# All 16 retention units in front of the first feed-forward layer

## Chip, cores and metric

The kernel runs on one core of a Trainium2 chip. The metric is the time of one execution on the device in microseconds (us), as the median of three runs. Engines are called PE (TensorE, the matrix engine), PEld (its weight loads, which overlap with it), DVE (VectorE), ACT (ScalarE), POOL (GpSimd) and SP (SyncE, which issues the DMAs).

## What is computed

A retention layer with 4 batches, 8 heads, 576 positions and 64 columns per head feeds two feed-forward layers over 2304 tokens of 512 columns, the first 2048 wide with a sigmoid gate, the second 1024 wide with a softmax, a product and a layer norm.

```python
def _attn_ref(q, k, v):
    scores = scale * np.matmul(q, k.transpose(0, 1, 3, 2))
    gamma = 1.0 - 2.0 ** (-5.0 - np.arange(H, dtype=np.float32))
    rel = pos[:, None] - pos[None, :]
    Dmat = np.where(rel >= 0, gamma[:, None, None] ** rel[None, :, :], 0.0)
    return np.matmul(scores * Dmat[None], v)
def _moe_ref(x, w_in, w_out):
    h = x @ w_in
    return (h * (1.0 / (1.0 + np.exp(-1.702 * h)))) @ w_out
def _moe2_ref(x, w_in, w_out, g_ln):
    h = x @ w_in
    solu = h * softmax(h)
    return (layer_norm(solu) * g_ln) @ w_out
```

## The kernel before

**Retention.** A unit is one batch and one pair of heads; there are 16. Its 576 positions are four chunks of 128 and a rest of 64. Within a chunk the scores k times q are computed directly and masked by a triangle; what earlier chunks contribute goes through a state of 64 x 64 per head, the sum of k times v over those chunks. The decay is carried by factors: v is multiplied by gamma to the minus position, the output by gamma to the position, over the whole 576 positions. The stages of a unit are `st0` (v times its factors, L308, on DVE for units 0, 1, 2 and 7, else on POOL), `st2` (scores, L356, and the two masks, L360), `states` (k times v of each chunk, L318, and the copy out by ACT, L327, into the two diagonal blocks of a 128 x 128 matrix per chunk), `st1` (running sums of the states over the chunks, L336, on DVE for units 0 to 2, else on POOL) and `st4` (states times q as full 128 x 128 matmuls, L376 and L380; masked scores times v, L385; the rest of 64 positions, L396; the scores of the next unit's rest, L344; and on DVE the output times its factors, L403 and L404). A table of output factors for 576 positions is grown on ACT from one for 128 (L197).

The stages of neighbouring units overlap: the scores of unit u come before `st4` of unit u - 1, and `st4` of u - 1 has the states of u in its middle. Inputs of a unit (128 x 2240 numbers) lie in one of six slots; when `st4` of a unit is written, the load of a later unit into its slot is issued on SP's queue.

**First layer.** 2304 tokens are six blocks of 384, and 2048 columns are two halves of eight slices. A step is one block and one slice: `emit_h` (12 matmuls, L439, then a sigmoid on ACT, L443, a product on DVE, L444, and a split of the result into a high part, L446 on ACT or L448 on DVE, and a low part, L449) and `emit_y` of the step before (12 matmuls, L470). Weights and tokens are split likewise, so that three products of rounded parts stand for one in full precision. Weights arrive as 64-bit numbers, 128 x 1024 words for half a slice. Six pieces on DVE (L224, L227, L230 for each half) convert a slice to 32 bits; then ACT casts the high part (L246) and POOL subtracts for the low part (L251, two instructions). `split_x` makes the parts of the tokens (L420 on ACT, L421 on POOL).

**What sets the order.** Each engine runs its instructions in the order in which the program writes them. Conversion pieces and the weight casts wait in a list, and `background(n)` writes n pieces of DVE and whatever follows them. The table `START` says how many pieces follow each stage and how many retention stages are written between the steps of the first block; later blocks take the rest in even portions. Units 0 to 3 come before the first step, the other twelve are spread over the first four blocks (`attend`).

**Second layer.** It starts after both halves of the first (L499 onwards) and isn't touched.

Of the kernel before, what the change touches and what calls it, by code (L numbers as in the profile page):

```python
# [9 lines left out]
F32 = mybir.dt.float32  # L10
F32R = mybir.dt.float32r
U32 = mybir.dt.uint32
# [33 lines left out]
for _name, _w in (  # L46
    ("vdec", NP * NV), ("tri", CH), ("tri2", LAST), ("half", 1), ("g_ln", FB), ("step", NP * NCH), ("qdec", NP * CH),
):
    _CC[_name] = (_n, _n + _w)
    _n += _w  # L50
# [3 lines left out]
def constants():  # L54
# [10 lines left out]
    step = np.zeros((P, NP, NCH))  # L65
    vdec = np.zeros((P, NP, NV))
    j = np.arange(P)
    for p in range(NP):
        g = gamma[2 * p + head_of_row][:, None]
        qdec[:, p] = g ** j[None, :]  # L70
        step[:, p] = g ** (CH * np.arange(1, NCH + 1)[None, :])
        for b in range(NCH):
            for a in range(2):
                vdec[:, p, 2 * b + a] = gamma[2 * p + a] ** (-(b * P + j))
        vdec[:, p, NV - 1] = gamma[2 * p + head_of_row] ** (-(NCH * CH + j % D))
# [17 lines left out]
for _name, _w in (  # L93
    ("c", _CC["qdec"][0]), ("qdec", NP * S), ("y", NB * KB * TB), ("g", 2 * TB), ("x", B * NP * S // 2),
    ("att", 2 * CATT + 2 * NCH * P + 4 * NCH * CH + 2 * LAST), ("t", SLICE),
):
    _M[_name] = _n
    _n += _w
# [3 lines left out]
IN_AT = [_M["att"], _M["att"] + CATT, _M["y"] + 3 * YT, _M["y"] + 3 * YT + CATT, CMEM, CMEM + 4 * S]  # L102
IN_OF = [0, 1, 2, 3, 4, 5, 0, 1, 2, 3, 0, 1, 2, 3, 0, 1]
ST_AT = _M["att"] + 2 * CATT
R1_AT = ST_AT + 2 * NCH * P
R2_AT = R1_AT + 4 * NCH * CH

T_START = [_M["t"], _M["y"] + 1 * YT, _M["y"] + 2 * YT]
# [13 lines left out]

START = {
    "warm": 10,
    "load": ["u1a", "u1b", "q", "u2a", "u2b", "u3a", "w0a", "u3b", "u4a", "w0b", "u4b", "w1a", "w1b", "u5a", "u5b", "w2a", "w2b", "w3a", "w3b", "w4a", "w4b"],
    "pre": [0, 0, 0, 0, 0, 1, 2, 0, 0, 2, 1, 3, 1],
    "ahead": [3],  # L130
    "step": [[2, 1, 2], [2, 1, 2], [2, 1, 2], [2, 1, 2], [2, 1, 2], [2, 2, 2], [2, 2, 2], [2, 0, 4]],
    "stages": [1, 0, 1, 0, 1, 1, 1, 1, 0, 2, 1, 1, 1, 1, 1, 1],
    "per_stage": 1,
    "lo_dve": [0, 0, 1, 0, 0, 0, 0, 0],
    "hi_act": [0, 1, 0, 0, 1, 0, 1, 1],
    "lo_at": [0, 4],
    "v_dve": [0, 1, 2, 7],
    "sum_dve": [0, 1, 2],
}


class Build:
# [37 lines left out]
    def load_qdec(self):  # L180

        nc = self.nc
        q = self.qdec()
        nc.sync.dma_start(
            out=q[:, :, 0:CH],
            in_=self.const_in[:, _CC["qdec"][0]:].rearrange("r (p i) -> r p i", p=NP),
        )

    def qdec(self):
        return self.at(_M["qdec"], NP * S).rearrange("r (p i) -> r p i", p=NP)  # L190

    def grow_qdec(self, p):
        q = self.qdec()
        for c in range(1, NCH + 1):
            n = min(CH, S - c * CH)
            f = self.const("step")[:, p * NCH + c - 1:p * NCH + c]
            self.nc.scalar.mul(q[:, p, c * CH:c * CH + n], q[:, p, 0:n], f)  # L197
# [5 lines left out]
    def load_unit(self, u, part=None):  # L203

        t = IN_AT[IN_OF[u]]
        a, b = {None: (0, CATT), 0: (0, 2 * CH), 1: (2 * CH, CKN), 2: (CKN, CATT), 3: (0, CKN)}[part]
        self.load(t + a, self.att_in[u, :, a:b])
# [57 lines left out]
    def stage(self, i, u):  # L265
        getattr(self, f"st{i}")(u)
        self.staged.add((i, u))

    def un(self, u):

        t = self.at(IN_AT[IN_OF[u]], CATT)
        st = self.at(ST_AT + (u % 2) * NCH * P, NCH * P).rearrange("r (c e) -> r c e", c=NCH)
# [10 lines left out]
    def qd(self, u):  # L283
        return self.qdec()[:, u % NP]

    def bank(self, name):
        return self.ps.tile([P, 512], F32, tag="s", name=name, bufs=4)

    def banks(self, u, name):

        if u < NP:
            t = self.ps.tile([P, 2, 512], F32, tag="y", name=f"{name}_{u}", bufs=2)
            return [t[:, a] for a in range(2)]
        return [self.bank(f"{name}{a}_{u}") for a in range(2)]
# [7 lines left out]
    def st0(self, u):  # L302

        v = self.un(u)[0][:, CV:CATT].rearrange("r (b e) -> r b e", b=NV)
        p = u % NP
        dec = self.const("vdec")[:, p * NV:(p + 1) * NV].unsqueeze(2).to_broadcast([P, NV, D])
        eng = self.nc.vector if u in START["v_dve"] else self.nc.gpsimd
        eng.tensor_tensor(v, v, dec, ALU.mult)  # L308

    def states(self, u):  # L310

# [12 lines left out]

        for a in range(2):
            r = slice(a * D, (a + 1) * D)
            nc.scalar.copy(st[r, :, r], pt[r, 0:NCH * D].rearrange("r (c e) -> r c e", c=NCH))  # L327

    def st1(self, u):

        if u == 0:
            self.states(0)
# [14 lines left out]
    def st2(self, u):  # L347
# [3 lines left out]
        s = self.banks(u, "s1")  # L351

        for c in range(NCH):
            for a in range(2):
                r = slice(a * D, (a + 1) * D)
                nc.tensor.matmul(  # L356
                    s[a][:, c * CH:(c + 1) * CH], self.k(t, c, r), self.q(t, c, r), start=True, stop=True
# [457 lines left out]
```

## Time and profile before

| | us |
|---|---|
| median of three runs | 736.18 (734.79 to 737.37) |
| the profiled execution | 738.06 |
| its span, first to last instruction | 736.30 |
| PE busy in the span | 711.4 (97%) |
| DVE, POOL, ACT busy | 445.1, 203.9, 185.8 |

PE is busy nearly throughout, but busy time is time with a matmul in flight at whatever clock the engine had. The granted clock is given per stretch as a share of 2.4 GHz; its two levels are 1.00 and 0.50 (1.2 GHz), and a value between is a mean. Rows of the timeline give the start and the duration of a run of instructions; a run that starts before the last one's end overlaps it, so costs are read from one start to the next. In the trace each matmul of the program shows as two instructions where both its operands are in 32-bit floating point (retention), and as one where they are split parts (the layers).

### The profile page before, as it was taken

What the parts mean: (1) busy time and instruction counts of PE and PEld (TensorE: products, weight loads), DVE (VectorE), ACT (ScalarE), POOL (GpSimd) and SP (SyncE); (2) the same over time, 40 slices, a digit from 0 to 9 for tenths busy, and PEclk for the clock granted to TensorE, in tenths of its full rate; (3) what the DMA queues carried; (4) which work ended last, traced back from release to release, by engine and by line L of the source; (5) the groups of instructions that cost most, each with busy time, mean ns of one, the idle gap of its engine ahead of it and who ended that gap; (6) DMA issues with size and microseconds to landing.
All of it is one profiled execution on the core that took longest, in us unless ns stands there. A gap on an engine that the chain in (4) does not pass through costs nothing.

```text
span 736.3 us, 10807 instructions
## 1 busy us (share of the span) xinstructions
PE 711.4 (97%) x4380; PEld 660.6 (90%) x4380; DVE 445.1 (60%) x745; ACT 185.8 (25%) x372; POOL 203.9 (28%) x211
## 2 busy tenths in 40 slices
PE   8888899999999999989999999999999999999998
PEld 7777799999999998989999999999878888888887
DVE  5899834443534789944676767655577454645451
ACT  3331231221212133412111111224323232222231
POOL 1576860312312026712021111137412111111000
PEclk9797999999999999999999999999999999999999
DMA  9980130111010333200112112000000000000001
GB/s 329 416 359 1 64 126 1 63 64 63 1 58 1 115 115 115 86 29 1 58 58 85 59 58 59 31 0 1 1 1 28 29 16 28 16 28 28 15 29 43
DMA packets 13392, 49.37 MB, mean 67 GB/s; under 512 B 1440, under 2 KB 2592, under 8 KB 11680
## 3 DMA queue, kind: packets, MB, share of 16 engines
q1 hardware_dynamic: 13344, 48.70, 18.3%
q8 instruction: 34, 0.56, 0.3%
q14 instruction: 14, 0.11, 0.0%
HBM read 43.97 MB, written 4.72 MB: 66 GB/s over the span
## 4 chain that ended last, share of the span: by engine, by line
PE 84%; DVE 12%; issue 2%; ACT 1%; DMA 1%; SPq 0%; POOL 0%; DVEq 0%; ACTq 0%
PE h L439 25%; PE yp L470 25%; PE o L561 14%; PE h L499 12%; PE zT L534 2%; DVE mem L224 2%; DVE mem L230 2%; PE o L385 2%; DVE wraw L227 2%; PE s L356 1%; PE o L376 1%; DVE gs L449 1%; PE T L318 1%; DVE mem L444 1%; DMA mem<-in_att 1%
## 5 line engine op out<-in xcount | busy, mean ns | idle before, releaser
L470 PE MATMUL yp<-gs,w 128*128 128x384 f32 x1152 | 222.6, 341 | 4.6 <-DVE gs L449 2.3
L439 PE MATMUL h<-xs,w 128*128 128x384 f32 x1152 | 224.2, 344 | 0.0
L470 PEld LDWEIGHTS yp<-gs,w 128*128 128x128 f32 x1152 | 205.7, 191 | 7.2 <-DVE gs L449 3.2
L439 PEld LDWEIGHTS h<-xs,w 128*128 128x128 f32 x1152 | 207.3, 191 | 1.1
L444 DVE TENSOR_TENSOR mem<-h,mem 128x384 f32<-128x384 f32 x96 | 53.4, 557 | 143.1 <-ACT mem L443 142.9
L443 ACT ACTIVATE mem<-h 128x384 f32<-128x384 f32 x96 | 47.3, 493 | 281.9 <-PE h L439 278.1
L561 PE MATMUL o<-w,zs 128*128 128x512 f32 (+1 forms) x456 | 105.3, 387 | 0.0
L499 PE MATMUL h<-w,ys 128*128 128x512 f32 x432 | 101.3, 391 | 1.0 <-DVE mem L516 0.8
L499 PEld LDWEIGHTS h<-w,ys 128*128 128x128 f32 x432 | 80.9, 188 | 19.0 <-DVE mem L516 1.0
L561 PEld LDWEIGHTS o<-w,zs 128*128 128x128 f32 x456 | 81.3, 188 | 17.2
L251 POOL TENSOR_TENSOR w<-mem,w 128x512 fp32r<-128x512 f32 x48 | 69.3, 1463 | 37.2 <-ACT w L246 35.6
L449 DVE TENSOR_TENSOR gs<-mem,gs 128x384 fp32r<-128x384 f32 x89 | 64.0, 719 | 8.9 <-DVE gs L448 0.5
L421 POOL TENSOR_TENSOR xs<-xb,xs 128x384 fp32r<-128x384 f32 (+1 forms) x32 | 27.7, 894 | 146.9 <-ACT xs L420 146.9
L421 POOL TENSOR_TENSOR xs<-mem,xs 128x384 fp32r<-128x384 f32 (+1 forms) x32 | 27.7, 886 | 113.3 <-ACT xs L420 113.3
L544 DVE TENSOR_TENSOR zs<-zT,zs 128x512 fp32r<-128x512 f32 x36 | 23.1, 684 | 46.9 <-ACT zs L543 46.9
L448 DVE CAST gs<-mem 128x384 fp32r<-128x384 f32 x92 | 45.6, 495 | 8.7
L522 POOL TENSOR_TENSOR mem<-mem 128x1 f32<-128x1 f32 x18 | 9.9, 550 | 122.3 <-DVE mem L521 122.3
L246 ACT CAST w<-mem 128x1024 fp32r<-128x1024 f32 x24 | 25.0, 1048 | 50.4 <-DVE mem L230 28.9
L515 DVE TENSOR_TENSOR mem<-h,mem 128x1024 f32<-128x1024 f32 x18 | 22.1, 1227 | 23.6 <-ACT mem L514 23.6
L487 POOL TENSOR_TENSOR ys<-mem,ys 128x512 fp32r<-128x512 f32 x18 | 23.8, 1320 | 43.1 <-ACT ys L486 43.1
L336 POOL TENSOR_TENSOR mem<-mem 128x128 f32<-128x128 f32 x39 | 22.2, 570 | 38.5 <-ACT mem L327 36.5
L514 ACT ACTIVATE mem<-h,mem 128x1024 f32<-128x1024 f32 x18 | 20.1, 1118 | 48.6 <-DVE mem L512 48.6
(80 smaller groups left out, 577.8 us busy)
## 6 DMA issues: line engine op xcount, KB each, us to landing
mem<-in_att SPq DMA_DIRECT2D x10, 1120.0 KB, 5.4
mem<-in_w SPq DMA_DIRECT2D x16, 512.0 KB, 3.7
wraw<-in_w SPq DMA_DIRECT2D x10, 512.0 KB, 10.6
out<-mem SPq DMA_DIRECT2D x17, 256.0 KB, 2.0
mem<-in_w2in SPq DMA_DIRECT2D x8, 512.0 KB, 3.8
mem<-in_w2out SPq DMA_DIRECT2D x8, 512.0 KB, 3.7
wraw<-in_w SPq DMA_DIRECT2D x3, 1024.0 KB, 16.0
mem<-in_att SPq DMA_DIRECT2D x4, 544.0 KB, 8.4
```

What stands on the lines that cost most here:

```text
L246: nc.scalar.copy(self.w[key][0], w)
L251: nc.gpsimd.tensor_tensor(lo[:, c], w[:, c], f32(hi[:, c]), ALU.subtract)
L421: nc.gpsimd.tensor_tensor(t[:, 1, done:done + n], x, f32(t[:, 0, done:done + n]), ALU.subtract)
L439: nc.tensor.matmul(h[:, 0:TB], a[:, w], x[:, b], start=(n == 0), stop=(n == 3 * KB - 1))
L443: nc.scalar.activation(g, h[:, 0:TB], AF.Sigmoid, scale=1.702)
L444: nc.vector.tensor_tensor(g, h[:, 0:TB], g, ALU.mult)
L448: nc.vector.tensor_copy(gs[:, 0], g)
L449: lo_engine.tensor_tensor(gs[:, 1], g, f32(gs[:, 0]), ALU.subtract)
L470: nc.tensor.matmul(o, a[:, w], gs[:, b], start=(first and i == 0), stop=(last and i == 2))
L487: nc.gpsimd.tensor_tensor(ys[:, 1], y, f32(ys[:, 0]), ALU.subtract)
L499: nc.tensor.matmul(h[:, n], ys[:, a, k], b[:, w], start=(i == 0), stop=(i == 3 * KB - 1))
L561: nc.tensor.matmul(o[:, 0:n], z[:, a, k], b[:, c:c + n], start=(k == 0 and i == 0), stop=(k == FB - 1 and i == 2),)
```

## The change

All 16 units are done before the first step of the first layer; `START`, `attend` and the grown table are gone. In each unit:

- The factors run within a chunk only. v of all chunks takes the same two columns of factors, multiplied on ACT in three instructions. The output takes one table of 128 columns for all chunks.
- The state of a chunk is scaled by gamma to the 128 when ACT copies it out, and the running sums on DVE multiply by that too (`scalar_tensor_tensor`), so that the state moves from chunk to chunk.
- States are kept as 64 columns without the empty blocks, and states times q runs as two 64 x 64 matmuls for each chunk, one for each head, in two quarters of the array. They stand behind the masked scores times v and the states of the next unit.
- Five slots in place of six; with each unit one half slice of weights is loaded. Two conversion pieces are written in each unit from the second on (`PIECES`), three in each step of the first block (`STEP`). All casts of the gated result in the first block are on ACT, all low parts on DVE.

```diff
-IN_OF = [0, 1, 2, 3, 4, 5, 0, 1, 2, 3, 0, 1, 2, 3, 0, 1]
+NU = 5
+IN_AT = [_M["att"], _M["att"] + CATT] + [_M["y"] + i * CATT for i in range(3)]
...
+PIECES = (1, 1, 0)
+STEP = (1, 1, 1)
...
     def st0(self, u):
-        eng = self.nc.vector if u in START["v_dve"] else self.nc.gpsimd
-        eng.tensor_tensor(v, v, dec, ALU.mult)
+        for a in range(2):
+            w = v[:, 0:n].rearrange("r (c a e) -> r a c e", a=2, e=D)[:, a]
+            self.nc.scalar.mul(w, w, d[:, a:a + 1])
+        self.nc.scalar.mul(v[:, n:], v[:, n:], d[:, 2:3])
...
-        for a in range(2):
-            r = slice(a * D, (a + 1) * D)
-            nc.scalar.copy(st[r, :, r], pt[r, 0:NCH * D].rearrange("r (c e) -> r c e", c=NCH))
+        nc.scalar.mul(
+            st, pt[:, 0:NCH * D].rearrange("r (c e) -> r c e", c=NCH),
+            self.const("step")[:, u % NP:u % NP + 1],
+        )
...
-        eng = self.nc.vector if u in START["sum_dve"] else self.nc.gpsimd
+        g = self.const("step")[:, u % NP:u % NP + 1]
         for c in range(1, NCH):
-            eng.tensor_tensor(st[:, c], st[:, c - 1], st[:, c], ALU.add)
+            self.nc.vector.scalar_tensor_tensor(st[:, c], st[:, c - 1], g, st[:, c], ALU.mult, ALU.add)
...
-        for c in range(1, NCH):
-            nc.tensor.matmul(
-                o[:, c * CH:(c + 1) * CH], st[:, c - 1], self.q(t, c),
-                start=(c == 1), stop=False, skip_group_check=True,
-            )
...
+        if u + 1 < B * NP:
+            self.states(u + 1)
+
+        for c in range(1, NCH):
+            for r in half:
+                nc.tensor.matmul(
+                    o[r, c * CH:(c + 1) * CH], st[r, c - 1], self.q(t, c, r),
...
+        last = B * NP - 1
...
+        for u in range(1, last + 2):
+            if u <= last:
+                self.st2(u)
+                if u > 1:
+                    self.background(PIECES[0])
+            self.st4(u - 1)
+            self.staged.add((4, u - 1))
+
+            if u - 1 + NU <= last:
+                self.load_unit(u - 1 + NU)
+            load_w()
+            if u > 1:
+                self.background(PIECES[1])
+            if u <= last:
+                self.st1(u)
+            if u < last:
+                self.st0(u + 1)
+            if u - 1 < NP:
+                self.split_x(0, 0, u - 1)
```

Two places of the order. First DVE from the masks of unit 3 (before) and unit 4 (after) on; s, o are scores and outputs in PSUM with the unit as first number, wraw is a raw weight slice. Before:

```order
L360 TENSOR_TENSOR mem<-s_3_275,mem 128x512 x2
L403 TENSOR_TENSOR mem<-o_2_286,mem 128x512
L404 TENSOR_TENSOR mem<-o_2_287,mem 128x64
L345 TENSOR_TENSOR mem<-o_2_287,mem 128x64
L224 TENSOR_SCALAR mem<-wraw_96 128x512
L227 SCALAR_TENSOR_TENSOR wraw_96<-wraw_96,mem 128x512
L230 SCALAR_TENSOR_TENSOR mem<-wraw_96 128x512
```

After (in the names of the change, s has no unit in its name here):

```order
L317 TENSOR_TENSOR mem<-s_324,mem 128x512 x2
L197 SCALAR_TENSOR_TENSOR wraw_91<-wraw_91,mem 128x512
L364 TENSOR_TENSOR mem<-o_3_336,mem 128x512
L369 TENSOR_TENSOR mem<-o_3_361,mem 128x64
L302 TENSOR_TENSOR mem<-o_3_361,mem 128x64
L200 SCALAR_TENSOR_TENSOR mem<-wraw_91 128x512
L293 SCALAR_TENSOR_TENSOR mem<-mem 128x64 x3
```

The pieces now stand one by one, before and behind the output scaling, and the three sums of every unit are on DVE.

Second ACT, in the unit in which the first weight slice is complete; T are states in PSUM, w a split weight, xs split tokens. Before:

```order
L420 CAST xs_0_2_320<-mem 128x384
L197 ACTIVATE mem<-mem 128x128 x3
L197 ACTIVATE mem<-mem 128x64
L246 CAST w_333<-mem 128x1024
L327 COPY mem<-T_366 64x4x64 x2
```

After:

```order
L283 ACTIVATE mem<-T_345,mem 128x256
L216 CAST w_374<-mem 128x1024
L265 ACTIVATE mem<-mem 128x4x64 x2
L266 ACTIVATE mem<-mem 128x64
L385 CAST xs_0_3_382<-mem 128x384
```

The scaling of v for the next unit (L265, L266) stands behind the cast of the weight, as it does in every third unit.

## Rows read from the trace of the kernel before

**Rows 1.** Windows by stage: length, busy us (instructions) per engine, clock, DMA share, GB/s.

```profile
9.46:90.24 80.78, 67.91 (x600) 61.46 (x597) 73.78 (x109) 24.70 (x52) 50.80 (x44) 0.83 0.59 234
90.24:226.00 135.76, 135.76 (x1102) 131.23 (x1101) 56.01 (x109) 30.37 (x74) 38.42 (x55) 1.00 0.15 51
226.00:510.30 284.30, 280.21 (x1572) 278.95 (x1569) 192.34 (x321) 64.71 (x132) 75.02 (x68) 0.99 0.17 56
```

**Rows 2.** Windows up to 226 us, line L439, then L470, alone (PE, PEld).

```profile
0.00:226.00 226.00, 72.74 (x361) 66.03 (x361) 0.94 0.33 126
...
0.00:226.00 226.00, 67.60 (x348) 61.80 (x348) 0.94 0.33 126
```

**Rows 3.** Timeline of PE, undisturbed steps: start, us, line, instructions.

```profile
242.99 2.28 PE L439 MATMUL h<-xs,w 128*128 128x384 f32 x12
...
247.22 2.28 PE L439 MATMUL h<-xs,w 128*128 128x384 f32 x12
```

**Rows 4.** Timeline of PE, two clean units and two waits [idle before it <- releaser].

```profile
13.81 1.16 PE L356 MATMUL s<-mem 64*128 64x128 f32 x16
14.90 0.94 PE L376 MATMUL o<-mem 128*128 128x128 f32 x6
...
16.56 1.10 PE L385 MATMUL o<-mem 128*64 128x128 f32 x16
17.49 0.63 PE L318 MATMUL T<-mem 128*64 128x64 f32 x16
18.06 0.33 PE L396 MATMUL o<-mem 64*64 64x64 f32 x4
...
18.43 1.16 PE L356 MATMUL s<-mem 64*128 64x128 f32 x16
...
22.36 1.23 PE L376 MATMUL o<-mem 128*128 128x128 f32 x4 [2.34 <-DVE mem L336]
...
58.15 1.09 PE L376 MATMUL o<-xb,mem 128*128 128x128 f32 x4 [1.24 <-POOL mem L336]
```

**Rows 5.** Windows of 2 us after the two waits, columns as in rows 1.

```profile
22.00:24.00 2.00, 1.64 (x8) 1.52 (x10) 1.93 (x5) 0.00 (x0) 0.16 (x1) 0.50 1.03 422
...
60.00:62.00 2.00, 1.88 (x16) 1.48 (x16) 2.00 (x2) 0.00 (x0) 1.98 (x2) 0.50 0.00 0
```

**Rows 6.** Timeline of DVE in unit 3.

```profile
17.87 0.41 DVE L224 TENSOR_SCALAR mem<-wraw 128x512 uint32<-128x512 uint32 x1
18.20 0.68 DVE L403 TENSOR_TENSOR mem<-o,mem 128x512 f32<-128x512 f32 x1
18.80 0.21 DVE L404 TENSOR_TENSOR mem<-o,mem 128x64 f32<-128x64 f32 x1
...
19.06 0.68 DVE L227 SCALAR_TENSOR_TENSOR wraw<-wraw,mem 128x512 uint32<-128x512 uint32 x1
19.78 1.37 DVE L230 SCALAR_TENSOR_TENSOR mem<-wraw 128x512 uint32<-128x512 uint32 x1
21.07 1.23 DVE L336 TENSOR_TENSOR mem<-mem 128x128 f32<-128x128 f32 x1
```

**Rows 7.** Timeline of POOL in the same stretch.

```profile
20.56 1.59 POOL L308 TENSOR_TENSOR mem<-mem 128x576 f32<-128x576 f32 x1
```

**Rows 8.** Lines L336 and L230 up to 60 us: duration ns min/median/max, starts, forms.

```profile
L336 DVE TENSOR_TENSOR mem<-mem x9: 293/294/1230, 10.5 to 22.7; 128x128 f32<-128x128 f32 x9
...
L230 DVE SCALAR_TENSOR_TENSOR mem<-wraw x9: 693/1374/1644, 19.8 to 56.1; 128x512 uint32<-128x512 uint32 x9
```

**Rows 9.** Timeline of ACT: four multiplications by a column, and the cast of a weight.

```profile
11.73 1.23 ACT L197 ACTIVATE mem<-mem 128x128 f32<-128x128 f32 x4 [1.32 <-DMA mem<-in_consts]
...
47.34 1.04 ACT L246 CAST w<-mem 128x1024 fp32r<-128x1024 f32 x1 [6.97 <-DVE mem L230]
```

**Rows 10.** Page, part 5: two groups, with busy us, mean ns, idle before.

```profile
L444 DVE TENSOR_TENSOR mem<-h,mem 128x384 f32<-128x384 f32 x96 | 53.4, 557 | 143.1 <-ACT mem L443 142.9
L449 DVE TENSOR_TENSOR gs<-mem,gs 128x384 fp32r<-128x384 f32 x89 | 64.0, 719 | 8.9 <-DVE gs L448 0.5
```

**Rows 11.** Timeline of PE behind a wait at 313 us.

```profile
315.38 3.52 PE L470 MATMUL yp<-gs,w 128*128 128x384 f32 x10 [0.86 <-DVE gs L449]
```

More of the change, by code (lines that the diff above doesn't have):

```diff
@@ L117 @@
 T_LATER[1] = T_LATER[1] + [OB_AT, U_AT + 2 * F2]
[L126 to L139, printed above, removed]
+PIECES = (1, 1, 0)
+STEP = (1, 1, 1)
+WARM = 10
 class Build:
@@ L180, in load_qdec @@
     def load_qdec(self):
[L182 to L186, printed above, removed]
-        )
[L189 to L197, printed above, removed]
+        lo, hi = _CC["qdec"]
+        self.load(_M["c"] + lo, self.const_in[:, lo:hi])
     def const(self, name):
@@ L393, in st4 @@
             self.states(u + 1)
-        for a in range(2):
-            r = slice(a * D, (a + 1) * D)
+        for c in range(1, NCH):
+            for r in half:
+                nc.tensor.matmul(
+                    o[r, c * CH:(c + 1) * CH], st[r, c - 1], self.q(t, c, r),
+                    start=False, stop=(c == NCH - 1), skip_group_check=True,
+                )
+        o2 = self.bank(f"o2_{u}")
+        for r in half:
+            nc.tensor.matmul(
+                o2[r, 0:LAST], st[r, NCH - 1], self.q(t, NCH, r),
+                start=True, stop=False, skip_group_check=True,
+            )
+        for r in half:
             nc.tensor.matmul(
@@ L584, in run @@
                 self.load_consts()
[L586 to L603 removed]
+        self.load_unit(1, 3)
+        self.load_qdec()
+        self.load_unit(1, 2)
+        for u in range(2, NU):
+            self.load_unit(u, 3)
+            self.load_unit(u, 2)
+            load_w()
         others = []
@@ L637, in run @@
-        cut = order.index((4, NP - 1)) + 1
-        pre = [sum(1 for i, _ in order[:n] if i) for n in range(cut)]
-        for n, (i, u) in enumerate(order[:cut]):
-            run_stage(i, u)
-            if i == 4:
-                self.split_x(0, 0, u)
-            if i:
-                self.background(START["pre"][pre[n]])
-        rest = order[cut:]
-        def attend(n, pieces=0):
-            while rest and (n > 0 or not rest[0][0]):
-                i, u = rest.pop(0)
-                run_stage(i, u)
-                if i:
-                    self.background(pieces)
-                    n -= 1
@@ L656, in run @@
-        for n in START["ahead"]:
-            attend(1, n)
-        stage_no = [s for s in rest if s[0]]
-        total = len(stage_no)
-        done = lambda: total - sum(1 for i, _ in rest if i)
-        goal = [None] + [stage_no.index((4, u)) + 1 for u in (9, 12)] + [total]
+        last = B * NP - 1
+        self.st0(0)
+        self.st2(0)
+        self.states(0)
+        self.st1(0)
+        self.st0(1)
+        for u in range(1, last + 2):
[7 more added lines that the diff above has]
+                self.load_unit(u - 1 + NU)
+            load_w()
+            if u > 1:
[6 more added lines that the diff above has]
+                self.split_x(0, 0, u - 1)
+            if u > 1:
+                self.background(PIECES[2])
@@ L676, in run @@
             if start:
-                attend(START["stages"][2 * fl], START["per_stage"])
-                self.background(START["step"][fl][0])
-            elif g == 0 and j < 4:
-                if fl == 0:
-                    before = done()
-                upto = lambda slot: before + -(-(goal[j] - before) * min(slot + 1, 14) // 14) - done()
-                attend(upto(2 * fl))
+                while f not in self.split:
+                    self.background(1)
+                self.background(STEP[0])
             if have_next and fl == FH - 2:
@@ L686, in run @@
                 self.split_x(*nextb, 1)
-            lo_pool = start and not START["lo_dve"][fl]
-            self.emit_h(g, j, f, nc.gpsimd if lo_pool else nc.vector, start and START["hi_act"][fl])
-            bg = START["step"][fl][1] if start else 2
+            self.emit_h(g, j, f, nc.vector, start)
+            bg = STEP[1] if start else 2
             if fl:
@@ L694, in run @@
                 self.split_x(*nextb, 3)
-            if start:
-                attend(START["stages"][2 * fl + 1], START["per_stage"])
-            elif g == 0 and j < 4:
-                attend(upto(2 * fl + 1))
             if prev is not None:
@@ L707, in run @@
                     held.pop(0)()
-            self.background((START["step"][fl][2] if start else 1) + (0 if fl else bg))
+            self.background((STEP[2] if start else 1) + (0 if fl else bg))
             if g == NH - 1 and last_block:
@@ L715, in run @@
             prev = (g, j, f)
-        assert not rest
         self.emit_y(*prev)
```

127 lines of the change are left out of this document (47 added, 80 removed).

## Prediction

> **What bounds the kernel now.** I read the busy time by stage first [rows 1]. From 90.24 us on, TensorE (PE) works without a gap: 135.76 of 135.76 us, then 280.21 of 284.30, at a granted clock of 1.00 and 0.99. In 9.46 to 90.24 it works 67.91 of 80.78 us at a mean clock of 0.83, while VectorE (DVE) is busy 73.78 of 80.78. So the tail is PE's own time, and the start is the only place where 10 us or more can be won. Second, how much of the start is the feed-forward layer. Up to 226.0 us (the stages are cut where the scores of unit 1 start, 9.46, and where the last retention matmul ends, 226.0) the trace has 30 groups of 12 matmuls of the h kind and 29 of the y kind (361 and 348 instructions [rows 2], one of them already in the next group). A step of h and y takes 247.22 - 242.99 = 4.23 us where nothing disturbs it [rows 3], so a group takes 2.115 us, and the 59 groups would take 59 x 2.115 = 124.8 us. **The rest, 226.0 - 124.8 = 101.2 us, is what the 16 retention units, the start and every loss cost today.** The changed kernel does the same 59 groups after its front, so it wins what its front (and any new loss in the first block) stays under 101.2 us. Everything behind 226.0 us has the same instructions in the same order, its own stall at 313 us included [rows 11], and is costed at no change.
>
> Third, why the start loses. Two units pass cleanly: the scores of unit 2 start at 13.81, those of unit 3 at 18.43 [rows 4]. Then PE waits 2.34 us for the running sums of the states (L336) and the granted clock falls to half: 0.50 in 22 to 24 us, and again 0.50 in 60 to 62 us after a wait of 1.24 us [rows 4, 5].
>
> **The change part by part.** *PE's work in a unit.* Scores 14.90 - 13.81 = 1.09 us; the masked scores times v 17.49 - 16.56 = 0.93; the states 18.06 - 17.49 = 0.57; the two pairs for the last 64 positions 18.43 - 18.06 = 0.37 [rows 4]. All four stay. Removed are three full 128x128 matmuls and one for the rest (0.94 us for the first six instructions). In their place come 6 quarter matmuls over 128 columns and 2 over 64. The trace has no quarter over 128 columns. Nearest is the half-width form of L385, 16 instructions in 0.93 us, which makes 12 cost 0.70; the full form, six in 0.94, would make them 1.9. I take 0.75, since L396 and L344, quarters over 64 columns, take 0.37 for eight and so are no dearer than the half-width form; by them the two short ones cost 0.19. Sum: 1.09 + 0.93 + 0.57 + 0.75 + 0.19 + 0.37 = 3.9, taken as 4.0 us a unit.
>
> *DVE's work in a unit.* The two masks cost as much as two of L403 (18.80 - 18.20 = 0.60 each), 1.20; the output scaling 0.60; the two short ones together 19.06 - 18.80 = 0.26 [rows 6]. The decay of v leaves DVE and POOL. The three sums become three scalar_tensor_tensor instructions on 64 columns, all on DVE. L336 on 128 columns takes 293 to 294 ns [rows 8]; the half-width form is between the 0.13 of a short one and that, I take 0.25, so 0.75. Two pieces of weight conversion ride along in each unit; L224 takes 18.20 - 17.87 = 0.33, L227 19.78 - 19.06 = 0.72 [rows 6], and and L230 0.69 at its fastest [rows 8], where the one at 19.78 took 1.37 with POOL beside it. The mean is 0.58, two are 1.16. Sum: 1.20 + 0.60 + 0.26 + 0.75 + 1.16 = 4.0 us. *DMA.* By the shapes in the code each unit asks for 128 x 2240 x 4 bytes of q, k and v and 128 x 1024 x 4 of weights, together 1.67 MB, and at the 422 GB/s of a full queue [rows 5] that is 3.96 us. Five slots instead of six let a load start four units ahead. **So three resources all need 4.0 us a unit, and none has slack to absorb a wait of another.**
>
> *ScalarE (ACT)* takes over v. Four of its multiplications by a column run in 1.23 us [rows 9], so 0.30 for 128 columns. A cast of 1024 takes 1.04, which with the first gives some 0.73 ns a column. Two over 256 columns are 2 x 0.40, the short one 0.26: 1.06 us a unit, hidden in the 4.0 as long as it starts on time. It does not in every third unit. The order shows the cast of a weight (L216 in the changed file, L246 before) in front of v of the next unit, and the cast waits for a conversion piece on DVE that stands behind the output scaling. Counted from the end T of the unit's matmuls: the piece is done at T + 0.9, the cast at T + 1.9, v at T + 3.1. PE wants v for the states of the next unit at T + 1.09 + 0.93 = T + 2.0. Four units (5, 8, 11, 14) therefore make PE wait some 1.2 us each, 5 us in all.
>
> *The clock.* Waits of this length have been followed by half clock [rows 4, 5], and one such spell stretched ten matmuls from 10 x 2.115 / 12 = 1.8 to 3.52 us [rows 11], a loss of 1.7 us. I cost three spells, 5 us.
>
> *The front.* It starts as before: scores of unit 1 at about 9.5 us, since DMA sets this. Then 15 units of 4.0 = 60, and the last without scores and states, 4.0 - 1.09 - 0.57 = 2.3. With waits and clock: 9.5 + 60 + 2.3 + 5 + 5 = **81.8 us**.
>
> *POOL.* It loses v and the sums, a part of the 50.80 us it is busy today in 9.46 to 90.24 [rows 1]. Left in the front are four splits of x and some nine half weights. A DVE instruction with two inputs in SBUF stretches beside POOL: L336 takes 293 ns at least and 1,230 at most [rows 8], and the longest begins at 21.07 us, inside POOL's instruction of 20.56 to 22.15 [rows 6, 7]. The Trainium skill ("SBUF — State Buffer", section "Who interferes with whom") says that such a pair takes an exclusive lock and that the later one stands still; this trace's 1,230 ns agrees, and the price of that is a rival below.
>
> *First block.* 29 of 48 pieces are done in the front, 19 are left, three a step. Beside the 1.3 us of a step's own DVE work (0.557 and 0.719 [rows 10]) that is 3 x 0.58 = 1.7, or up to 3.5 beside POOL, in a step of 4.23: it fits, but the last weight is cast in the step before it is needed, and behind it on ACT stand four casts of the next x and the sigmoid of step 6. I cost 4 us here, with 0 and 9 as the ends. Sum: 81.8 + 4 = 85.8 against 101.2, a gain of 15.4 us.
>
> **The rivals.** *Cleaner.* The waits come but the clock holds and the first block hides its casts: 71.8 + 5 = 77 us, 24 less than 101.2. For it: the unit from 13.81 to 18.43 took 4.62 us with its small waits in it, and no half clock followed until the 2.34 us. Against: 1.24 us was enough once [rows 5]. Time 712. *DVE is held up by POOL.* A POOL instruction on 576 columns took 1.59 us [rows 7], so nine half weights of 512 columns at 1.4 and four splits of x of 384 at 1.06 are some 17 us of POOL time, an estimate; if DVE stands still for most of it, and DVE is already at 4.0 a unit, 14 us come on top and the gain is gone: 735. Against it: the masks and scalings read PSUM, and only the pieces and sums, some half of DVE's time, can be caught. The exclusive lock of the Trainium skill's page "SBUF — State Buffer" is the rule that speaks for this one. *Slower: the clock stays low in the front.* The small matmuls leave gaps whenever DVE, DMA or ACT slips, and at half clock a unit costs 8.0 instead of 4.0; 22 to 24 us of today ran so [rows 5]. Break-even is 15.4 us, four units more at half clock than costed. With half of the units so (8 x 4.0 = 32 in place of my 5) the front is 109 and the time 748. For it: mean clock 0.83 in today's start. Against: the waits of 2.34 and 1.24 us were for the sums L336 [rows 4], on DVE behind POOL's v or on POOL itself, and the change takes both off POOL. *Slower: quarters do not pair.* At the full form's 0.157 an instruction the 16 quarters of a unit cost 2.5 instead of 0.94, 25 us in all, less the 5 of waits that this would hide: 741. That the order is not what the words say is ruled out by the listing of both orders.
>
> **How the numbers follow.** The profiled execution took 738.06 us (span 736.30 and 1.76 around it), 1.88 above the median of the runs, 736.18. 738.06 - 15.4 - 1.88 = 720.8 us. Chances: forecast 0.58, cleaner 0.15, POOL 0.10, low clock 0.13, unpaired quarters 0.04. The range reaches from 711 (cleaner) to 738 (POOL, and a clock low for some six units) and leaves out most of the last two cases, 0.17, and little else. A difference under 0.3% (2.2 us) can't be told from none. Half of the POOL case falls within it: faster 0.78, same 0.06, slower 0.16.
>
> **What would show it.** Right: the first h matmul starts between 78 and 88 us, scores follow each other every 4.0 us with about 5.2 at units 5, 8, 11 and 14, where PE waits for ACT's scaling of v; PE's clock in the front averages 0.9 or more; the first block takes 34 to 43 us. Wrong: scores 5 us or more apart in every unit (then the name of the engine PE waits for tells whether it is POOL's lock, DMA or the quarters), a clock under 0.8 in the front, PE waits of several us at steps 5 to 7 of the first block, or a tail behind the first block that is not the same to within 2 us.

## The result and the profile after

The changed kernel takes **718.36 us** (716.53 to 720.27) against 736.4 us measured beside it, a ratio of 0.9757 (95% interval 0.9726 to 0.9789). The prediction was 720.8 us, faster. The profiled execution took 717.78 us, with a span of 716.0 us.

The page of the changed kernel gives the busy time per engine, with its share of the span and the number of instructions:

```profile
PE 694.4 (97%) x4508; PEld 643.8 (90%) x4508; DVE 440.3 (61%) x783; ACT 197.7 (28%) x392; POOL 155.1 (22%) x152
```

PE's busy share is 97% as before; what fell is its busy time, from 711.4 to 694.4 us. The mean clock of the start, 0.83 in [rows 1], is gone, as the windows of the changed kernel show (columns as in [rows 1]):

```profile
0.00:40.00 40.00, 36.05 (x560) 31.80 (x560) 28.07 (x68) 17.91 (x39) 7.46 (x10) 1.00 0.97 379
40.00:80.00 40.00, 35.85 (x613) 31.77 (x614) 35.36 (x89) 16.23 (x35) 8.03 (x6) 0.96 0.75 303
```

The two profiled executions differ by 738.06 - 717.78 = 20.3 us. Cut at the same two points of the work:

| stretch | before | after | difference |
|---|---|---|---|
| to the start of the 31st group of h | 226.00 | 209.31 | -16.7 |
| from there to the first matmul of the second layer | 290.33 | 287.85 | -2.5 |
| second layer, to the end of the span | 219.97 | 218.84 | -1.1 |

The first stretch is the one that the prediction priced, at -15.4. The other two it priced at nothing; they gave 3.6 us.

The timeline of PE (start, us, line, instructions, [idle before <- releaser]) shows the longest wait of the front with the slow quarters behind it, then a clean unit, then the end of the front:

```profile
43.58 0.33 PE L277 MATMUL T<-mem 128*64 128x64 f32 x2 [1.32 <-ACT mem L265]
...
45.04 1.55 PE L346 MATMUL o<-mem 64*64 64x128 f32 x12
...
60.16 1.16 PE L313 MATMUL s<-mem 64*128 64x128 f32 x16
...
62.74 0.87 PE L346 MATMUL o<-mem 64*64 64x128 f32 x12
63.45 0.28 PE L352 MATMUL o<-mem 64*64 64x64 f32 x4
63.56 0.28 PE L357 MATMUL o<-mem 64*64 64x64 f32 x4
...
63.89 0.38 PE L313 MATMUL s<-mem 64*128 64x128 f32 x2
...
79.79 4.46 PE L404 MATMUL h<-xs,w 128*128 128x384 f32 x24
```

A clean unit takes 63.89 - 60.16 = 3.73 us. Its twelve instructions of quarters over 128 columns take 63.45 - 62.74 = 0.71, the four over 64 take 0.11. Behind the wait the row of the twelve lasts 1.55 us in place of 0.87, at half clock (below). The first h starts at 79.79 us. What PE waits for up to 80 us (us in total, times, longest):

```profile
PE T L277 <- ACT mem L265: 4.7, 10, 1.3
PE s L313 <- DMA mem<-in_att: 1.9, 3, 1.0
...
PE o L346 <- DVE mem L293: 0.2, 1, 0.2
```

The waits on the running sums, 2.34 and 1.24 us in [rows 4], have all but gone; the largest in total is now the one for ACT's scaling of v, L265, as forecast.

### The profile page after: what moved, and what is told of

Read it like the earlier page. It is cut to its first block, busy times and chain, and to the rows that moved or that the text cites. A ratio compares the mean times of both kernels' runs of the same rounds, so it can differ in the third digit from the quotient of the medians.

```text
span 716.0 us, 11014 instructions
## 1 busy us (share of the span) xinstructions
PE 694.4 (97%) x4508; PEld 643.8 (90%) x4508; DVE 440.3 (61%) x783; ACT 197.7 (28%) x392; POOL 155.1 (22%) x152
## 4 chain that ended last, share of the span: by engine, by line
PE 78%; DVE 13%; ACT 3%; issue 3%; DMA 2%; POOL 1%; SPq 0%; DVEq 0%; POOLq 0%; ACTq 0%
PE h L404 24%; PE yp L435 24%; PE o L526 14%; PE h L464 12%; DMA mem<-in_att 2%; DVE mem L200 2%; PE zT L499 2%; DVE wraw L197 1%; DVE mem L194 1%; DVE mem L317 1%; DVE mem L409 1%; DVE mem L197 1%; DVE mem L293 1%; PE o L346 1%; ACT w L216 1%
## 5 line engine op out<-in xcount | busy, mean ns | idle before, releaser
L404 PE MATMUL h<-xs,w 128*128 128x384 f32 x1152 | 217.3, 337 | 1.2 <-POOL w L221 0.9
L435 PEld LDWEIGHTS yp<-gs,w 128*128 128x128 f32 x1152 | 202.8, 188 | 12.3 <-DVE gs L414 8.0
L404 PEld LDWEIGHTS h<-xs,w 128*128 128x128 f32 x1152 | 202.2, 188 | 2.4 <-POOL w L221 1.2
L221 POOL TENSOR_TENSOR w<-mem,w 128x512 fp32r<-128x512 f32 x48 | 65.2, 1382 | 97.1 <-ACT w L216 97.1
L414 DVE TENSOR_TENSOR gs<-mem,gs 128x384 fp32r<-128x384 f32 x96 | 71.9, 749 | 13.5 <-ACT gs L411 4.1
L413 DVE CAST gs<-mem 128x384 fp32r<-128x384 f32 x88 | 43.2, 491 | 8.8
L451 ACT CAST ys<-mem 128x512 fp32r<-128x512 f32 x18 | 11.2, 621 | 58.9 <-PE h L464 58.9
```

What stands on the lines that cost most here:

```text
L221: nc.gpsimd.tensor_tensor(lo[:, c], w[:, c], f32(hi[:, c]), ALU.subtract)
L404: nc.tensor.matmul(h[:, 0:TB], a[:, w], x[:, b], start=(n == 0), stop=(n == 3 * KB - 1))
L413: nc.vector.tensor_copy(gs[:, 0], g)
L414: lo_engine.tensor_tensor(gs[:, 1], g, f32(gs[:, 0]), ALU.subtract)
L435: nc.tensor.matmul(o, a[:, w], gs[:, b], start=(first and i == 0), stop=(last and i == 2))
```

## The experiments

Each ratio is to the kernel before, measured on the same chip in the same series; differences in us are (1 - ratio) x 736.2. Intervals are 95%.

### The units alone, the order alone

The change has two parts: cheaper units, and all of them in front. The first kernel has the new units in the order of before, the second the old units in the order of the change. Both keep the weights where they lay before in SBUF.

```diff
 # old_order_new_units: the units of the change ...
+        self.nc.scalar.mul(v[:, n:], v[:, n:], d[:, 2:3])
+            self.nc.vector.scalar_tensor_tensor(st[:, c], st[:, c - 1], g, st[:, c], ALU.mult, ALU.add)
+                    o[r, c * CH:(c + 1) * CH], st[r, c - 1], self.q(t, c, r),
 # ... with START and attend of the kernel before
```

> The units of the change (v scaled on ScalarE, decay within chunks, compact states, quarters, all sums on DVE) in the order of the kernel before: units 0 to 3 in front, the others between the steps of the first four blocks; the tile behind which the weights lie keeps its old size. Theory (the gain comes from both: POOL's sums and v made PE wait in the start, and the retention between the first steps left DVE no time for weights): the waits for sums of 2.34 and 1.24 us go, the first block still loses by conversion pieces; about 728 us, half of the gain of 18. Rival 1 (the units alone are the gain): 720 or less. Rival 2 (the order alone is the gain): 734 to 738.

Measured: 731.33 us, ratio 0.9925 (0.9905 to 0.9945), so -5.5 us: slower than the 728 expected, faster than the 734 of the second rival. The timeline of PE at its two longest waits:

```profile
28.09 1.52 PE L305 MATMUL T<-xb 128*64 128x64 f32 x16 [4.00 <-ACT xb L293]
...
56.30 0.69 PE L305 MATMUL T<-mem 128*64 128x64 f32 x16 [3.81 <-DVE mem L439]
```

The units are cheaper, but in the old order the states (L305) wait three times for more than 3 us: once, 4.00 us, for v (L293), which stands on ACT behind the cast of a weight, and twice until the product of h on DVE (L439) is done, 3.81 us here and 3.29 at 73.38.

```diff
 # new_order_old_units: the order of the change (NU, PIECES, STEP), with
+        eng = self.nc.vector if u in (0, 1, 2, 7) else self.nc.gpsimd
+        eng.tensor_tensor(v, v, dec, ALU.mult)
...
+        eng = self.nc.vector if u in (0, 1, 2) else self.nc.gpsimd
+            eng.tensor_tensor(st[:, c], st[:, c - 1], st[:, c], ALU.add)
```

> The order of the change (all 16 units in front, five slots, one piece behind the scores and one behind the output of each unit) with the units of the kernel before: v on POOL but for units 0, 1, 2 and 7, sums on POOL from unit 3 on, 128-wide states, full matmuls of states times q in front of the masked scores times v. Theory: states times q stands right behind the scores, so PE waits for POOL's sums in every unit, 1.5 us or more, and the clock falls with it: units of 6 to 8 us, the front ends at 100 to 120 us, 738 to 755 us in all. Rival (the order alone is the gain): about 720 us, units of 4.5 us at most.

Measured: 727.06 us, ratio 0.9865 (0.9844 to 0.9887), so -9.9 us. **This expectation was missed.** It took the long waits of before to be the old units' own and to come again in every unit. A window of that kernel (columns as in [rows 1]), and its PE at one unit and at the first h:

```profile
40.00:80.00 40.00, 38.62 (x518) 31.55 (x516) 30.66 (x60) 9.10 (x19) 31.72 (x40) 1.00 0.79 304
```

```profile
43.20 1.16 PE L329 MATMUL s<-mem 64*128 64x128 f32 x16
44.29 1.38 PE L349 MATMUL o<-mem 128*128 128x128 f32 x6
48.09 1.16 PE L329 MATMUL s<-mem 64*128 64x128 f32 x16
...
86.18 4.50 PE L412 MATMUL h<-xs,w 128*128 128x384 f32 x24
```

POOL is busy 31.72 of 40 us, and states times q come stretched (1.38 where six took 0.94 in [rows 4]), but a unit takes 48.09 - 43.20 = 4.89 us, from the first scores to the first h PE never waits more than 1.0 us at a time, and the clock stays at 1.00. So the long waits of [rows 4] and the half clock behind them belonged to the order of before, in which units, steps of the layer and pieces share each engine's line of work; the new units alone left three long waits standing there. Each part removes what the other leaves: the order the long waits, the new units some 5.6 us of the front (first h at 86.18 us here, at 80.59 with the new units and the weights in the same place, the next kernel). A clean new unit is over one us shorter, 3.73 us, but with its waits a unit takes 4.7 us in the mean there in place of 4.9; most of the rest of the 5.6 comes behind the last scores.

### The weights' place in SBUF

The compact states and tables make the big array in front of the weights 9,360 bytes shorter, so the weights begin at byte 110592 of each partition in place of 119936 (9,344 lower, as starts are rounded). To see whether the 3.6 us behind the first cut come from there, the array gets its old length back, with columns that nothing uses.

```diff
-CMEM = _n
+CMEM = _n + 2340
```

> The changed kernel with 2340 unused columns at the end of the large tile, so that the weights lie where they lay in the kernel before; nothing else is changed. A group of 12 h matmuls took 2.09 us in the changed kernel and 2.115 in the one before. Theory (the place of the weights in SBUF sets this): 2.115 us again, about 2 to 3 us more in all than the changed kernel, 720 to 721. Rival (it comes from something else in the change): 2.09 us and 718.

Measured: 721.61 us, ratio 0.9792 (0.9763 to 0.9821). The timelines of PE in undisturbed steps, first with the old place, then the changed kernel:

```profile
240.19 2.28 PE L404 MATMUL h<-xs,w 128*128 128x384 f32 x12
242.30 2.27 PE L435 MATMUL yp<-gs,w 128*128 128x384 f32 x12
244.41 2.28 PE L404 MATMUL h<-xs,w 128*128 128x384 f32 x12
```

```profile
242.91 2.25 PE L404 MATMUL h<-xs,w 128*128 128x384 f32 x12
245.00 2.27 PE L435 MATMUL yp<-gs,w 128*128 128x384 f32 x12
247.11 2.25 PE L404 MATMUL h<-xs,w 128*128 128x384 f32 x12
```

The step is 4.22 us at the old place, as the 4.23 of [rows 3], and 4.20 at the new one, and all of it is in h: 242.30 - 240.19 = 2.11 against 245.00 - 242.91 = 2.09. So an edit that was to save memory sped up matmuls that it does not touch. The ratio moves by 0.0035, 2.6 us; the intervals of the two overlap, the rows of the trace do not.

How much of the 3.6 us this is, the stretches behind the first cut tell. The second layer takes 219.9 to 220.0 us in the four kernels with the old place (that of before, the two of the last section, and this one) and 218.8 in the changed kernel, so its 1.1 us are the place. The middle stretch is mixed. In the kernel before the granted clock falls in it twice, at 295 and at 315 us [rows 11], and in this one twice too, at 280 and at 301; it takes 290.33 and 291.05 us. In the changed kernel it doesn't fall there, though waits come (its middle stretch is 287.85 us). First a window of the kernel before (columns as in [rows 1]), then the longest wait there in PE's timeline of the changed kernel:

```profile
296.00:298.00 2.00, 2.00 (x8) 2.00 (x7) 1.76 (x5) 1.28 (x2) 0.15 (x1) 0.50 0.54 172
```

```profile
292.91 0.62 PE L435 MATMUL yp<-gs,w 128*128 128x384 f32 x2 [1.50 <-DVE gs L413]
294.46 2.00 PE L435 MATMUL yp<-gs,w 128*128 128x384 f32 x10 [0.93 <-DVE gs L414]
```

The old units in the new order have the old place and no fall at all, and take 288.52 us. So of the 2.5 us of the middle stretch some 0.7 go with the place and some 1.8 with the two spells of half clock; why these stay away isn't shown (two other executions with the old length kept a mean clock of 1.00, so it is not the place alone). The new place also speeds up the 30 groups of h ahead of the first cut.

With the place held, the parts add up within their intervals: -5.5 (units) and -9.9 (order) make -15.4, and the two together are (1 - 0.9792) x 736.2 = -15.3.

Three more lengths were to find which places are good, with 16, 128 and 1024 unused columns.

> The changed kernel with 16 unused columns (64 bytes of each partition) ahead of the weights, so that these begin at byte 110656 in place of 110592. Theory (what counts is whether the weights begin at a multiple of 256 bytes or more): a step of h goes back from 2.09 to 2.115 us, the time to some 721.6. Rival (it is the place as a whole, 9,344 bytes lower than before, that counts): h stays at 2.09, 718.4.

> The same with 128 unused columns: the weights begin at 111104, a multiple of 512 bytes but not of 1024. Theory (multiple of 256 bytes or more): h stays at 2.09 and the time at 718.4; if only larger multiples help, 2.115 and 721.6. Rival (place as a whole): 718.4 here and with 16 columns alike.

> The same with 1024 unused columns: the weights begin at 114688, a multiple of 4096 bytes as in the changed kernel, but nearly halfway to the old place. Theory (multiple of 256 bytes or more): 2.09 and 718.4. Rival (place as a whole): between the two, a step of h at 2.10 and 720.

Measured: 719.98, 717.46 and 718.28 us, ratios 0.9783 (0.9761 to 0.9806), 0.9751 (0.9725 to 0.9777), 0.9759 (0.9739 to 0.9779); all three intervals overlap that of the changed kernel, so the rows decide. With 128 and 1024 columns h and y keep the changed kernel's 2.09 and 2.11 us. With 16 columns, 64 bytes, the timeline is

```profile
242.41 2.28 PE L404 MATMUL h<-xs,w 128*128 128x384 f32 x12
244.53 2.25 PE L435 MATMUL yp<-gs,w 128*128 128x384 f32 x12
246.61 2.28 PE L404 MATMUL h<-xs,w 128*128 128x384 f32 x12
```

64 bytes are enough to slow h to 2.12, so it is not the region that counts. But y, unforeseen, became faster, 246.61 - 244.53 = 2.08. Since gs, which y reads, had moved by the same 64 bytes, it was moved with the weights left in place, on top of the kernel of the next section (there 715.08 us):

```diff
         self.wp = pool("wp")
+        self.gap = pool("gap").tile([P, 16], F32, name="gap")
```

> The kernel with v scaled first (715.08 us), with 16 unused columns behind the weights, so that these stay at byte 110592 and the gated result gs (which y reads) begins at 176192 in place of 176128. Theory (the 16 columns ahead of the weights made y faster, 2.08 in place of 2.11 us, through the place of gs, and h slower, 2.12 in place of 2.09, through that of the weights): h 2.09, y 2.08, and with 96 steps the time falls by 96 x 0.03 = 2.9 us to 712. Rival (y became faster through the place of its weights): h 2.09, y 2.11, 715.1 as without it.

Measured: 715.76 us, ratio 0.9731 (0.9714 to 0.9747). The timeline in the first layer, and one group of h in the second:

```profile
244.90 2.25 PE L436 MATMUL yp<-gs,w 128*128 128x384 f32 x12
246.99 2.25 PE L405 MATMUL h<-xs,w 128*128 128x384 f32 x12
...
643.16 5.77 PE L465 MATMUL h<-w,ys 128*128 128x512 f32 x24
648.77 1.04 PE L500 MATMUL zT<-mem 128*128 128x128 f32 x8
```

The mechanism was right, y now takes 246.99 - 244.90 = 2.09 with the weights where they were. The time of 712 was missed (the interval overlaps that of the kernel without the gap): the 64 bytes also moved ys, which the second layer reads, and its h takes 648.77 - 643.16 = 5.61 us, where the kernel without the gap has, in the same groups,

```profile
644.08 5.61 PE L464 MATMUL h<-w,ys 128*128 128x512 f32 x24
649.52 1.04 PE L499 MATMUL zT<-mem 128*128 128x128 f32 x8
```

5.44. Eighteen groups lose 18 x 0.17 = 3.1 us, more than the 96 x 0.02 = 1.9 that y wins (2.11 - 2.09).

### The wait on ACT

The forecast had v wait on ACT behind the cast of a weight. If that is what costs, v of the next unit must come ahead of the piece that the cast waits for.

```diff
             load_w()
+            if u < last:
+                self.st0(u + 1)
             if u > 1:
                 self.background(PIECES[1])
             if u <= last:
                 self.st1(u)
-            if u < last:
-                self.st0(u + 1)
```

> The changed kernel with the scaling of v of the next unit written ahead of the second conversion piece, so that on ScalarE it stands in front of the cast of the weight. Theory: PE's waits for ScalarE's scaling of v at units 5, 8, 11 and 14 (0.4, 1.5, 1.0 and 1.4 us in the trace) and the spell of half clock behind unit 8 go, and the front ends some 4 us earlier, at 75 to 77 us; 714 to 715 us in all. Rival (the loads set the front, at 1.67 MB a unit): PE waits as long for q and k instead, the front ends within 1 us of 79.8, and the time stays at 717 to 718.

Measured: **715.08 us**, ratio 0.9697 (0.9675 to 0.972), the best of all here. PE's waits on ACT up to 80 us (us in total, times, longest), and the first h in the timeline:

```profile
PE T L277 <- ACT mem L265: 0.6, 3, 0.2
```

```profile
76.36 1.83 PE L404 MATMUL h<-xs,w 128*128 128x384 f32 x9
```

The wait on v falls from 4.7 to 0.6 us, and the first h comes 3.4 us earlier. The half-clock spell of the front is gone too, and the 714 to 715 us expected came.

The other way out is another engine. This kernel scales v on POOL:

```diff
-            self.nc.scalar.mul(w, w, d[:, a:a + 1])
-        self.nc.scalar.mul(v[:, n:], v[:, n:], d[:, 2:3])
+            self.nc.gpsimd.tensor_scalar_mul(w, w, d[:, a:a + 1])
+        self.nc.gpsimd.tensor_scalar_mul(v[:, n:], v[:, n:], d[:, 2:3])
```

> The changed kernel with the scaling of v on POOL in place of ScalarE (three multiplications by a column). ScalarE's cast is then in front of nothing, but POOL gets some 2 us more in each unit, and DVE's pieces and sums with two inputs in SBUF stretch beside it. Theory: DVE, level with PE at 4.0 us a unit, becomes the bound; units of 4.6 to 5.0 us, the front ends at 84 to 90 us, 723 to 728 us. Rival (masks and output scalings read PSUM and leave enough room): the waits for ScalarE are gone and nothing replaces them, 714 to 716.

Measured: 720.29 us, ratio 0.9781 (0.9762 to 0.9799), between the two expectations. PE's waits for v (us in total, times, longest):

```profile
PE T L277 <- POOL mem L265: 8.5, 10, 1.3
```

The wait moves to POOL and nearly doubles, from 4.7 to 8.5 us: one multiplication of 256 columns takes 0.94 us here in the median and 0.51 on ACT, and they share the queue with the low weights. The first h comes at 80.45 us, not at 84 to 90 as the theory had it. Moving the call within ACT's queue took the wait away; moving it to another busy queue did not.

### The pieces of weight conversion

With no pieces in the units (the work is not left out, it runs behind them), the front shows what it can do at most. Only its front is read.

```diff
-PIECES = (1, 1, 0)
+PIECES = (0, 0, 0)
```

> The changed kernel without conversion pieces in the front; all 48 are left to the first block, which will wait for them (some 25 to 30 us), so only the front is read. Theory (PE, DVE and DMA are level at 4.0 us a unit): without 1.2 us of pieces DVE is off the path, and no cast stands in front of v, but the loads still arrive at 4.0 us a unit; the first h could start at 73 to 76 us in place of 79.8. Rival 1 (DMA sets the front alone): 78 or more. Rival 2 (DVE alone was the bound): PE's own 3.75 us a unit, 70 or less.

Measured, in a single execution: 738.53 us in all. The timeline of PE and a window:

```profile
55.57 1.16 PE L313 MATMUL s<-mem 64*128 64x128 f32 x16 [0.15 <-DMA mem<-in_att]
...
59.53 1.16 PE L313 MATMUL s<-mem 64*128 64x128 f32 x16 [0.15 <-DMA mem<-in_att]
...
78.64 0.69 PE L404 MATMUL h<-xs,w 128*128 128x384 f32 x1 [5.33 <-ACT w L216]
```

```profile
40.00:60.00 20.00, 19.26 (x368) 17.63 (x368) 14.83 (x44) 8.95 (x21) 0.00 (x0) 1.00 1.02 419
```

Units follow each other every 59.53 - 55.57 = 3.96 us and wait for their loads, at 419 GB/s. That is the 3.96 that the prediction worked out from 1.67 MB and 422 GB/s. Retention ends at 73.3 us; the first h comes only at 78.64 because it waits 5.33 us for a weight whose pieces were put off, so it is the 73.3 that answers the expectation, in favour of its theory. The kernel with v first is 3 us above that, with the pieces done.

With no piece ahead of a step's h in the first block, three behind it and one at the step's end, in place of one at each, the waits there were to go:

```diff
-STEP = (1, 1, 1)
+STEP = (0, 3, 1)
```

> The changed kernel with the conversion pieces of the first block written as none ahead of a step's h, three behind its h and its gated result, one at its end (in place of one at each), so that no weight cast stands in front of a sigmoid on ScalarE and the last slice is done one step earlier. Theory: the losses of the first block (in the trace 0.87, 0.66 and 0.66 us of waits for the low part of the gated result with as much again around each, 0.9 for a weight and 0.3 for x, 5.6 us against a dense block) go: 4 to 5 us less, 713.5 to 714.5 us. Rival (DVE is the bound in the block, whatever the order): the waits move, within 1 us of 718.4.

> The scaling of v ahead of the second piece, as in st0_first, and the pieces of the first block as in step031. Theory: the two gains add, since they lie in different stages: 715.1 - 4 = 711 us. Rival: a gain in the front arrives with fewer pieces or loads done and is given back in the first block: 713 to 715.

Measured: 718.5 us, ratio 0.9751 (0.9733 to 0.977), and with v first 715.82 us, 0.9711 (0.9693 to 0.973): no gain beside 0.9757 and 0.9697. The expectations of 713.5 to 714.5 and of 711 were missed; the first one's rival, that the waits move, came. The timeline of PE in the first block, without v first:

```profile
92.95 0.62 PE L435 MATMUL yp<-gs,w 128*128 128x384 f32 x2 [1.20 <-ACT gs L411]
...
109.40 3.19 PE L435 MATMUL yp<-gs,w 128*128 128x384 f32 x10 [0.85 <-DVE gs L414]
```

The waits moved: now ACT's cast of gs comes 1.20 us late, which it did not in the changed kernel, and ten matmuls took 3.19 us in place of 2.01, with the granted clock at 0.50 in 110 to 112 us. From the first h to the tenth the block took 43.2 us in place of 41.3. The first h came at 78.78 us, a us earlier than without the edit; that is not the edit's doing, since the front has the same instructions and in this execution no spell of half clock (below). The rival's reason isn't shown: DVE is busy for 25.9 us of the block's 43.2.

## Why the prediction was right, and where its terms were off

**The frame held.** The gain was sought in the start alone, as 101.2 us less the front and the loss of the first block. By the cuts above that came out at 16.7, forecast 15.4. The sum closes: the front was 2.0 us shorter than forecast, the first block lost 1.6 more, and the 59 groups took 2.10 us each in place of 2.115, 0.9 in all.

**The front: 79.79 forecast 81.8.** It began at 8.74 us (forecast 9.5). The 14 units up to the last scores, at 73.26, took 64.52 (forecast 14 x 4.0 + 10 = 66), the last 6.53 (6.3). Nearly right, but with other terms, and in part by luck: 14 clean units of 3.73 would be 52.2 us, so 12.3 were lost beside them, 10 forecast, and the 3.8 by which the clean unit was priced too high paid for that. The terms:

- *PE's own work* is 3.73 us in a clean unit, not the 4.0 that was rounded up from 3.9. The quarters cost 0.71 and 0.11, forecast 0.75 and 0.19: the half-width form of [rows 4] was the right neighbour, and that rules out the rival of unpaired quarters.
- *ACT.* The place, the releaser and the total were right, the split was not. Four waits of 1.2 us, 5 in all, were forecast; ten came, 4.7 in all, the longest at units 8 (1.32), 11 (0.77) and 14 (1.14), each with a 0.22 behind it, and hardly any at 5 (0.17 and 0.21), where PE itself had just waited 1.02 for its loads. ACT's own rows at unit 11 show what was argued:

```profile
56.34 1.05 ACT L216 CAST w<-mem 128x1024 fp32r<-128x1024 f32 x1 [2.01 <-DVE mem L200]
57.29 1.06 ACT L265 ACTIVATE mem<-mem 128x256 f32<-128x256 f32 x2
58.25 0.34 ACT L266 ACTIVATE mem<-mem 128x64 f32<-128x64 f32 x1
```

  The cast waits 2.01 us for the piece L200, and v stands behind it. Scaling v takes 58.59 - 57.29 = 1.30 us, where 1.06 was forecast: from the forecast's rows [rows 9] the slope is (1.04 - 0.31) / 896 us, 0.82 ns a column and not 0.73, and even that gives only 1.08. That the waits come from this place in the queue is shown by the run with v first.
- *DMA* was said to have no slack, and then no wait was costed for it: 1.9 us in three waits.
- *The clock.* Three spells of 1.7 us were costed; there was one. Columns as in [rows 1]:

```profile
42.00:44.00 2.00, 0.58 (x8) 0.20 (x4) 1.93 (x7) 1.90 (x4) 0.81 (x1) 1.00 1.04 435
44.00:46.00 2.00, 1.88 (x24) 1.76 (x26) 0.74 (x2) 1.17 (x4) 1.86 (x2) 0.58 0.98 396
```

  It follows PE's longest idle time in the front, 1.32 us. The 1.14 at 70.96 and the 1.02 at 26.75 were followed by no fall: the two windows behind each show 1.00. The length of the wait alone does not decide: in the run with `STEP` changed, whose front has the same instructions, the same wait was 1.31 us and the clock stayed at 1.00.

```profile
43.72 0.33 PE L277 MATMUL T<-mem 128*64 128x64 f32 x2 [1.31 <-ACT mem L265]
```

```profile
44.00:46.00 2.00, 1.78 (x39) 1.62 (x38) 1.08 (x3) 1.44 (x5) 2.00 (x2) 1.00 1.00 407
```

  So whether a spell follows such a wait differs from run to run. The rival of a clock that stays low did not come. The long waits for the sums, behind which it had been low, are gone with the order: the old units in the new order kept 1.00 too.

**DVE and POOL.** The sums cost 0.92 us for three in a clean unit, 0.75 was taken. The rival in which POOL holds DVE up did not come, though its mechanism shows. DVE's timeline at two sets of running sums, then POOL's at the first of them, a subtraction for a low weight:

```profile
33.01 1.93 DVE L293 SCALAR_TENSOR_TENSOR mem<-mem 128x64 f32<-128x64 f32 x3
...
61.40 0.92 DVE L293 SCALAR_TENSOR_TENSOR mem<-mem 128x64 f32<-128x64 f32 x3
```

```profile
31.27 2.95 POOL L221 TENSOR_TENSOR w<-mem,w 128x512 fp32r<-128x512 f32 x2
```

The three sums that run into POOL's instruction take 1.93 in place of 0.92. This agrees with the exclusive lock of the Trainium skill ("SBUF — State Buffer", section "Who interferes with whom"). But over the front the median of a sum is 286 ns and the longest 1,289: of the sixteen sets this one alone met POOL. The 17 us of POOL time with which the prediction weighed that rival were about right (7.46 + 8.03 in the first 80 us); that DVE would stand still for most of it was not.

**The first block: 5.6 forecast 4.** From 79.79 to the tenth h at 121.11 there are 17 groups, 41.3 us, where 17 x 2.10 = 35.7 would do. The timeline of PE:

```profile
85.78 2.01 PE L435 MATMUL yp<-gs,w 128*128 128x384 f32 x10 [0.87 <-DVE gs L414]
...
112.04 2.19 PE L404 MATMUL h<-xs,w 128*128 128x384 f32 x11 [0.90 <-POOL w L221]
```

The forecast looked for waits of some us on ACT's casts at steps 5 to 7. What came is spread: DVE's low part of gs comes 0.66 to 0.87 late three times, at every second step, and POOL's low weight once by 0.90. The step that failed is that 1.3 us of DVE's own and 1.7 to 3.5 of pieces "fit" in 4.23: the work fits (DVE is busy for 25.1 of the 41.3 us), but not ahead of the part that PE wants next.

**Behind the front: 3.6 us, forecast nothing.** The prediction's last sentence allowed the tail 2 us, so by its own test this was wrong. Its premise, the same instructions in the same order, was true and not enough. Two things differ, as the runs on the place of the weights show: the 66 groups of h left are 0.02 to 0.03 us faster each, those of h in the second layer 0.04, which is the place, some 1.8 us of the 3.6 together; and the kernel before has two spells of half clock there that the changed kernel has not, the other 1.8. The stall at 313 us was one of the two, and it was costed as unchanged. In the profiled executions the forecast was 1.3 + 3.6 = 4.9 us too slow; in the medians it is 2.4 (720.8 against 718.36), by chance, because the profiled execution of before lay 1.88 above its median and that of the changed kernel 0.58 below.

## What to carry to other kernels

Read a wait by what stands ahead of the late instruction in its engine's queue: one moved call won 3 to 4 us here, and the same work on another engine won nothing. Units of one kind in a row kept PE from the longest waits and, but for one spell, from half clock, with the old dear units and the new cheap ones alike, where mixing them with a layer and its conversions had not: try the order before the arithmetic. And when a change alters how much memory lies ahead of a matmul's operands, compare the duration of one untouched matmul group before and after, before explaining the rest.

## What the runs showed of the hardware

The pace of a group of matmuls depended on where its operands begin in SBUF, in steps as small as 64 bytes: h took 2.09 us with the weights at byte 110592, 111104 or 114688 and 2.11 to 2.12 at 110656 and 119936; y took 2.11 with gs at 176128 and 2.08 to 2.09 at 176192, with the weights at either of two places; h of the second layer took 5.44 or 5.61 as ys moved by 64 bytes with the weights held, and 5.48 where both had moved by 64 (16 columns ahead of the weights). It isn't the multiple alone that decides, as what slowed one group sped up another; which rule joins the two operands' places stays open.

The granted clock fell to half behind one idle time of 1.32 us (0.58 in 44 to 46 us and 0.57 in 46 to 48, then 1.00 again) and did not behind idle times of 1.02, 1.14 and, at 292.91 us, 1.50 in the same execution; in the kernel before it had been 0.50 behind one of 1.24 [rows 4, 5]. At the place of the 1.32, the same instructions waited 1.31 us in the run with `STEP` changed and 1.97 in the one with 16 unused columns, and the clock stayed at 1.00. So in these runs the length of the idle time did not settle it; what does stays open.
